# Identity built on chip, state rows first, two output blocks formed in place, sums respaced

## The chip, the cores and the metric

The kernel runs on one core of a Trainium2 chip. The metric is the device time of one execution in microseconds (us). Each core has five engines with queues of their own: TensorE (PE, with its weight loads PEld), VectorE (DVE), ScalarE (ACT), GpSimd (POOL) and SyncE (SP). They meet at semaphores. Transfers are issued from the queues of SP, ACT and POOL.

## The reference

Two operators follow each other. The first is a cross attention between 512 tokens and 32 state rows of each of 8 heads in each of 8 batches, in both directions; the second is a feed-forward layer over its 4352 output rows.

```python
B, H, S, Ns, D = (8, 8, 512, 32, 64)
a  = softmax(scale * x @ state.T);  xread = a  @ state
a2 = softmax(scale * state @ x.T);  sread = a2 @ x
rows = concatenate([xread, sread], axis=2)      # (B, H, 544, 64)
X = rows.transpose(0, 2, 1, 3).reshape(B * 544, 512)
h = X @ w_in                                    # d_ff = 2048
g = s * relu(h) ** 2 + b
out = g @ w_out                                 # float32
```

The scalar b only adds b times the column sums of w_out to every row. The kernel adds that as bias_bc.

## The kernel before

All work of a batch is done in tiles with 128 partitions, matmuls in fp16 with fp32 accumulation. Eight heads form two groups g of four (`head_of`).

*Attention.* The tokens of a batch (xn) are transposed to xT by TensorE for batches 0 and 1 (`att_xT_pe`, 16 transposes with the identity matrix ident16 as the moving operand, then copies to SBUF on VectorE, L197, and ScalarE) and by a DMA transpose for the others. The state rows are transposed in the same manner to stT (`att_stT`, copy at L157). `att_T` forms the scores T from stT and xT and their exponentials E. `att_D` multiplies E by the block matrix bones16, which gives the softmax denominators, and forms the shares a4. `att_M` folds the state rows into w_in: M = state times w_in, so that the layer's h comes straight from a4 and M (`mm1_x`, sixteen tiles f of 128 hidden units; two matmuls each). ScalarE applies the relu (L395). VectorE squares pairs of tiles into g (L405), but in batch 1 two pairs are squared by ScalarE (L403).

*Start.* For batch 0, x comes in two transfers xf (one per group) on SP's queue, the state rows of batch 0 and 1 in two transfers stf, one on ACT's queue and one on SP's. The matrix ident16 is an inline constant that ACT's queue loads first (L713). Each of these is cast to fp16: xf in four quarters (`cast_x0`, L742, on VectorE, ScalarE, VectorE and POOL), stf by POOL (`cast_st`, L734). POOL issues the transfers that cast while moving: four wi (w_in), four wo (w_out), xn of later batches, the remaining state rows. TensorE multiplies zeros (`warm_up`) until x is there, and between its first steps.

*Second matmul.* The first half of batch 0's tokens is multiplied by w_out directly (`mm2_part`). The other half of batch 0 ("0b") and every later batch use a 2 x 2 block scheme with seven products instead of eight (`fast_items`). Tokens are cut in two halves, hidden units in two, and output columns in two. `weight_sums` gives the differences t1 to t4 of w_out blocks (wd, eight VectorE subtractions, L490); `token_sum(b, i, j)` gives the sums s1 to s4 of g blocks, in two parts j each (L507 for i = 3, L512, L514, L516). The products p = 1 to 7 accumulate in three PSUM banks A, B and C. When a product is complete, `done` lets VectorE read the bank:

```python
p == 1: qa = A * s + bias          # L605
p == 6: u2 = B * s + qa            # L608
p == 7: u3 = B * s + qa            # L613;  qb = qa + bias_d   L616
p == 2: put("A", blk(0), 0, 0)     # osb = A * s + bias        L572
p == 5: put("C", u3, 1, NH)
p == 4: put("B", qb, 1, 0)
p == 3: put("C", u2, 0, NH)
```

Product 7 goes on adding into bank B after product 6, and product 4 after product 7. Each `put` writes an output block osb (a pool of three buffers), and POOL issues its transfer to out.

*Order.* TensorE, SP and POOL run in the order in which the program writes them down (`manual_schedule`); VectorE and ScalarE are placed by the scheduler, except where `issue_after` ties an instruction to another. The work is in stages: stage s runs `mm1_x(s, f)` for f = 0 to 15; beside them stand pieces of the attention of batch s + 1 (`pieces`) and the products of batch s - 1 (`items`). Stage 1 takes the rest of batch 0, at first direct units, then "0b" in f = 6 to 13. A dictionary in stage 1 says after which f the weight differences (`sums.pop(0)`) and the sums of "0b" are issued. G["last"] is the latest square or direct output on VectorE.

Of the kernel before, what the change touches and what calls it, by code (L numbers as in the profile page):

```python
# [14 lines left out]
def kernel(  # L15
# [72 lines left out]

    warm = konst.tile([P, 512], FP16, name="warm")
    ident16 = konst.tile([P, P], FP16, name="ident16")  # L90
    ident_dr = nc.inline_tensor(np.eye(P, dtype=np.float16), name="ident_const")
    bones16 = konst.tile([P, P], FP16, name="bones16")
    ones16 = konst.tile([P, Ns], FP16, name="ones16")
    mean16 = konst.tile([P, P], FP16, name="mean16")
# [77 lines left out]
    def new_xT(b):  # L172
        A[b]["xT"] = apool.tile([P, H, 2, P], FP16, name=f"xT_{b}", tag="xT")
        return A[b]["xT"]

    def att_xT_pe(b, g):
# [16 lines left out]
        xT = A[b]["xT"] if g else new_xT(b)  # L193
        dst = xT.rearrange("p (q g) k t -> p g q (k t)", g=NG)[:, g]
        for i in range(2):
            eng = nc.scalar.copy if i == 1 and (b, g) != (0, 1) else nc.vector.tensor_copy
            eng(  # L197
                dst[:, h2 * i : h2 * i + h2],
                two[i].rearrange("p (q t) -> p q t", q=h2),
            )  # L200

    def att_xT_dma(b):
        xT = new_xT(b)
# [184 lines left out]
    def mm1_close(key, hps, ntok, f):  # L388
        if f % 2 == 0:
            R2[key] = rpool.tile([P, 2, ntok], FP16, name=f"r_{key}_{f}", tag="r")  # L390
        r16 = R2[key]
        if key == 0 and f in (1, 5):
            nc.vector.tensor_scalar(r16[:, f % 2], hps, 0.0, None, ALU.max)
        else:
            nc.scalar.activation(r16[:, f % 2], hps, AF.Relu)  # L395
            G["relu"] = nc.cur_bb.bb.instructions[-1]
        if f % 4 == 0:
            G4[key, f // 4] = gpool.tile([P, 4, ntok], FP16, name=f"g_{key}_{f}", tag="g")
        gt = G4[key, f // 4]
        G[key, f] = gt[:, f % 4]  # L400
        if key == 1 and f in (5, 9):
            with tc.issue_after(nc.cur_bb.bb.instructions[-1]):
                nc.scalar.square(gt[:, f % 4 - 1 : f % 4 + 1], r16)  # L403
        elif f % 2 == 1:
            nc.vector.tensor_mul(gt[:, f % 4 - 1 : f % 4 + 1], r16, r16)  # L405
            G["last"] = nc.cur_bb.bb.instructions[-1]
# [111 lines left out]
    def fast_items(b):  # L518
# [41 lines left out]
        def put(bank, add, j, n0):  # L560
            if b == "sr":
                ends.append(own[1][:, len(ends) : len(ends) + 1])
                osb = ends[-1]
            else:
                osb = opool.tile([P, ni, NH], FP32, name=f"osb_{b}_{j}_{n0}", tag="osb")
            if bank == "C" and b == last_b:
# [35 lines left out]
        def done(p):  # L602
            if p == 1:
                q = keep("qa")
                nc.vector.scalar_tensor_tensor(q, acc["A"], s_bc, blk(NH), ALU.mult, ALU.add)  # L605
            elif p == 6:
                u = keep("u2")
                nc.vector.scalar_tensor_tensor(u, acc["B"], s_bc, kept["qa"], ALU.mult, ALU.add)  # L608
            elif p == 2:
                put("A", blk(0), 0, 0)  # L610
            elif p == 7:
                u = keep("u3")
                nc.vector.scalar_tensor_tensor(u, acc["B"], s_bc, kept["qa"], ALU.mult, ALU.add)  # L613
                d = bias_d.unsqueeze(1).broadcast_to([P, ni, NH])
# [43 lines left out]
    def bias_sum():  # L658
# [11 lines left out]
                )  # L670
        nc.vector.tensor_copy(wsum[:, 0], ps)
        nc.vector.tensor_sub(wsum[:, 1], ps, wsum[:, 0])
        A["wsum"] = wsum

    def bias_end():
# [34 lines left out]

    with tc.manual_schedule(engines={ET.PE, ET.SP, ET.Pool}):
        nc.vector.memset(warm, 0.0)
        nc.scalar.dma_start(ident16, ident_dr.ap())  # L713
        for g in range(NG):
            nc.sync.dma_start(
                xf[:, g],
                x[0, g :: NG].rearrange("h (q c) d -> q h (c d)", q=P),
            )
        nc.scalar.dma_start(stf[:, 0:2, :], st_v[:, 0:2, :])
        nc.scalar.preload_act_table_set("natural_log_exp_and_others")  # L720
        nc.sync.dma_start(stf[:, 2:4, :], st_v[:, 2:4, :])
        nc.sync.dma_start(sb_row[:, 0:1], moe_s.to_broadcast((1, 1)))
# [1 line left out]
        nc.gpsimd.memset(bones16, 0.0)  # L724
        for q in range(4):
            nc.gpsimd.memset(bones16[32 * q : 32 * q + 32, 32 * q : 32 * q + 32], 1.0)
        nc.gpsimd.memset(ones16, 1.0)
        nc.gpsimd.memset(mean16, 1.0 / Ns)
        nc.gpsimd.memset(one_row, 1.0)

        def cast_st(eng, b0, b1):
            n = 2 * (b1 - b0)
# [21 lines left out]
        nc.gpsimd.dma_start(out=st16[:, 4:, 0, :], in_=st_v[:, 4:, :])  # L754
        load_x(2)

        warm_up(11)
        cast_x0(0, 0, nc.vector.tensor_copy)
        cast_x0(0, 1, nc.scalar.copy)
        att_xT_pe(0, 0)  # L760
        att_stT(0)
        cast_x0(1, 0, nc.vector.tensor_copy)
        warm_up(2)
        att_T(0, [0])
        att_xT_pe(0, 1)
# [111 lines left out]
        for s in range(1, B):  # L877
# [16 lines left out]
            for f in range(NKF):  # L894
# [7 lines left out]
                if s > 1 and f in (4, 5):  # L902
                    with tc.issue_after(G["last"]):
                        token_sum(s - 1, 4, f - 4)
                if s in fast:
                    if f in ((10, 12) if s == 1 else (7, 11)):
                        with tc.issue_after(G["last"]):
                            token_sum(s, 3, int(f > 10))
                    if s == 1 and f in (13, 14):
                        with tc.issue_after(G["last"]):  # L910
                            token_sum(s, f - 12, 0)
                    if s > 1 and f in (11, 12):
                        token_sum(s, f - 10, 0)
                    if f == 15:
                        token_sum(s, 1, 1)
                        token_sum(s, 2, 1)
                for fn in todo_s.get(f, []):
                    fn()
                if s == 1:
                    with tc.issue_after(G["last"]):  # L920
                        for _ in range({0: 2, 1: 1, 2: 1, 6: 1, 7: 1, 8: 1, 9: 1}.get(f, 0)):
                            sums.pop(0)()
                        for i, j in {0: [(1, 0), (2, 0)], 1: [(1, 1), (2, 1)], 7: [(3, 0)], 8: [(3, 1)],
                                     10: [(4, 0), (4, 1)]}.get(f, []):
                            token_sum("0b", i, j)
                for fn in items[f]:
                    fn()
        rest = coming[last_b][16:]
        rows = fast_items("sr")

# [53 lines left out]
```

The softmax here doesn't subtract the row's maximum and nothing guards it: scores larger than these inputs give would overflow.

## Time and profile before

| What | Value |
|---|---|
| median of 4 executions | 209.08 us (208.62 to 209.66) |
| profiled execution | 209.45 us, of it 207.7 us from first to last instruction |
| TensorE busy | 197.9 us, 1971 matmuls |
| VectorE busy | 163.4 us, 286 instructions |
| ScalarE busy | 128.4 us |
| POOL busy | 38.7 us |
| granted TensorE clock | 0.998 |
| HBM | 17.33 MB read, 8.91 MB written |

Starts are counted in us from the first instruction. A timeline line gives start, duration, engine, line of the program, operation, the tiles written and read, shapes and count; in square brackets stands how long the engine had been idle, and what released it. A helper's line number (L70 for every matmul) says little, so matmuls are told by their tiles: h is `mm1_x`, T and D the attention, Mps `att_M`, oA, oB and oC the three banks of products, each with the batch's name behind it where it is 0b or sr (the state rows' output).

### The profile page before, as it was taken

The numbers are of one execution on the slowest core, as the hardware profiler recorded it, in microseconds if no ns is written. First come the engines' busy times: TensorE is split into PE (matmuls) and PEld (weight loads), VectorE is DVE, ScalarE is ACT, GpSimd is POOL, SyncE is SP. The second block draws the span as 40 slices with busy tenths as digits, with TensorE's granted clock in tenths as the row PEclk, the third lists the DMA queues.
The fourth block names the chain that finished last, engine by engine and source line by source line (L and its number), as shares of the span: only waits on it lengthen the run. The fifth ranks groups of instructions, "written<-read, shape, count | busy, mean of one in ns | idle before, by whom it ended". The sixth has DMA issues, their size and how long they took to land.

```text
span 207.7 us, 4853 instructions
## 1 busy us (share of the span) xinstructions
PE 197.9 (95%) x1971; PEld 132.5 (64%) x1971; DVE 163.4 (79%) x286; ACT 128.4 (62%) x254; POOL 38.7 (19%) x66
## 2 busy tenths in 40 slices
PE   7788899999999999999999999999999999999991
PEld 2334343556766676667676667676767777788881
DVE  0479779896959996799779966997699786796861
ACT  2478975699677666767676658675867555543100
POOL 5591001413210230023002101120112012100210
PEclk9999999999999999999999999999999999999999
DMA  5999997999999496929951934160416011200243
GB/s 177 226 201 206 206 191 104 181 189 176 158 157 191 101 179 92 200 73 208 139 103 54 151 109 104 51 158 3 101 47 157 11 51 51 103 2 0 79 139 92
DMA packets 46795, 25.55 MB, mean 123 GB/s; under 512 B 31732, under 2 KB 44788, under 8 KB 46772
## 3 DMA queue, kind: packets, MB, share of 16 engines
q0 software_dynamic: 15568, 16.19, 39.7%
q1 hardware_dynamic: 30180, 8.49, 23.9%
q10 hardware_dynamic: 1024, 0.56, 1.0%
q8 instruction: 15, 0.25, 0.5%
q14 instruction: 8, 0.07, 0.1%
HBM read 17.33 MB, written 8.91 MB: 126 GB/s over the span
## 4 chain that ended last, share of the span: by engine, by line
PE 84%; DMA 5%; DVE 3%; ACT 3%; issue 1%; POOL 1%; ACTq 0%
PE h L70 24%; PE oB L70 18%; PE oC L70 11%; PE oA L70 11%; PE Mps L70 4%; PE o L70 3%; PE h_sr L70 3%; DMA stf<-in_state_dram 3%; DMA a<-aT 2%; ACT r L395 2%; PE V L70 1%; PE oB_sr L70 1%; PE T L70 1%; PE oB_0b L70 1%; DVE M L320 1%
## 5 line engine op out<-in xcount | busy, mean ns | idle before, releaser
L395 ACT ACTIVATE r<-h 128x512 f16<-128x512 f32 x126 | 74.2, 602 | 44.2 <-PE h L70 44.2
L70 PE MATMUL h<-a,M 128*128 128x512 f16 x256 | 74.2, 379 | 1.2 <-DVE M L320 0.6
L70 PEld LDWEIGHTS <-s 128*128 128x128 f16 x448 | 43.7, 98 | 15.8
L405 DVE TENSOR_TENSOR g<-r 128x1024 f16<-128x1024 f16 x62 | 42.3, 683 | 12.3 <-ACT r L395 11.6
L70 PEld LDWEIGHTS <-g 128*128 128x128 f16 x392 | 37.3, 98 | 18.5 <-issue 4.4
L583 POOL DMA_DIRECT2D out_dram<-osb x27 | 18.2, 674 | 123.6 <-DVE osb L572 51.6
L70 PE MATMUL oB<-wd,s 128*128 128x256 f16 x224 | 32.8, 273 | 0.0
L70 PE MATMUL oA<-wo,g 128*128 128x256 f16 x224 | 32.5, 273 | 0.0
L70 PEld LDWEIGHTS <-M 128*128 128x128 f16 x256 | 24.3, 98 | 11.4 <-DVE M L320 1.6
L297 ACT CAST M<-Mps 128x1024 f16<-128x1024 f32 x20 | 20.1, 1006 | 0.0
L70 PE MATMUL oC<-wd,s 128*128 128x256 f16 x112 | 16.5, 273 | 0.0
L70 PE MATMUL oB<-wd,g 128*128 128x256 f16 x112 | 15.7, 273 | 0.0
L70 PE MATMUL oC<-wo,s 128*128 128x256 f16 x112 | 15.3, 273 | 0.0
L608 DVE SCALAR_TENSOR_TENSOR u<-oB,s_bc,qa 128x512 f32<-128x512 f32 x7 | 5.2, 750 | 7.5 <-PE oB L70 7.5
L395 ACT ACTIVATE r_sr<-h_sr 128x256 f16<-128x256 f32 x16 | 6.1, 382 | 7.9 <-PE h_sr L70 7.3
L234 ACT ACTIVATE E<-T 128x256 f16<-128x256 f32 x20 | 7.4, 384 | 4.0 <-PE T L70 4.0
L514 DVE TENSOR_TENSOR s<-s,g 128x1024 f16<-128x1024 f16 x14 | 9.6, 687 | 0.2
L70 PE MATMUL h_sr<-srdT,wi 128*128 128x256 f16 x64 | 9.6, 273 | 0.0
L507 DVE TENSOR_TENSOR s<-g 128x1024 f16<-128x1024 f16 x14 | 9.6, 686 | 0.0
L516 DVE TENSOR_TENSOR s<-g,s 128x1024 f16<-128x1024 f16 x14 | 9.6, 685 | 0.0
L512 DVE TENSOR_TENSOR s<-g,g 128x1024 f16<-128x1024 f16 x14 | 9.6, 684 | 0.0
L572 DVE SCALAR_TENSOR_TENSOR osb<-oC,s_bc,u 128x512 f32<-128x512 f32 x12 | 8.9, 745 | 0.4 <-PE oC L70 0.4
(126 smaller groups left out, 224.8 us busy)
## 6 DMA issues: line engine op xcount, KB each, us to landing
out_dram<-osb POOLq DMA_DIRECT2D x29, 256.0 KB, 2.8
xn<-in_x_dram POOLq DMA_DIRECT2D x7, 512.0 KB, 7.8
wi<-in_moe_w_in_dram POOLq DMA_DIRECT2D x4, 512.0 KB, 8.9
wo<-in_moe_w_out_dram POOLq DMA_DIRECT2D x4, 512.0 KB, 14.5
xf<-in_x_dram SPq DMA_DIRECT2D x2, 512.0 KB, 5.5
out_dram<-osb_0b POOLq DMA_DIRECT2D x4, 128.0 KB, 5.3
out_dram<-osb_sr SPq DMA_DIRECT2D x8, 32.0 KB, 1.6
out_dram<-osb_sr ACTq DMA_DIRECT2D x8, 32.0 KB, 1.7
```

What stands on the lines that cost most here:

```text
L70: return nc.tensor.matmul(out, lhsT, rhs, start=start, stop=stop, tile_position=tp, is_transpose=is_transpose, skip_group_check=True,)
L234: nc.scalar.activation(a["E"][:, g, 256 * m : 256 * m + 256], Ts[m][:, g, :], AF.Exp, scale=scale, accum_out=a["rs"][:, NG * m + g : NG * ...
L297: nc.scalar.copy(dst, ps)
L395: nc.scalar.activation(r16[:, f % 2], hps, AF.Relu)
L405: nc.vector.tensor_mul(gt[:, f % 4 - 1 : f % 4 + 1], r16, r16)
L507: nc.vector.tensor_sub(o, a11, a21)
L512: nc.vector.tensor_add(o, a21, a22)
L514: nc.vector.tensor_sub(o, SQ[b, 1, j], a11)
L516: nc.vector.tensor_sub(o, a12, SQ[b, 2, j])
L572: nc.vector.scalar_tensor_tensor(osb, acc[bank], s_bc, add, ALU.mult, ALU.add)
L583: nc.gpsimd.dma_start(dst[j][:, :, n0 : n0 + NH], osb)
L608: nc.vector.scalar_tensor_tensor(u, acc["B"], s_bc, kept["qa"], ALU.mult, ALU.add)
```

## The change

It has three parts. The identity is no longer loaded: VectorE writes 0 to 31 along the free axis by doubling, transposes it in 32 x 32 blocks, and compares the two in the four diagonal blocks of a zeroed tile. ACT's queue issues stf's first transfer before anything else. TensorE transposes the state rows of batch 0 after nine warm-up matmuls, ahead of two more and of xT; VectorE's cast of the second half of xf is tied behind its first xT copy. Three POOL memsets change places. Second, `put` for output rows j = 1 writes its result over the operand added (u3 or qb), and the transfer to out reads that tile. Third, ScalarE's two squares of batch 1 are those of f = 3 and 5 instead of 5 and 9; the weight differences, third and fourth sums of "0b" are issued at other f, two of them tied behind u2 and u3; the third sums of batch 1 move from stage 1 (f = 10, 12) to stage 2 (f = 1, 2).

```diff
-    ident_dr = nc.inline_tensor(np.eye(P, dtype=np.float16), name="ident_const")
+    lane_c = konst.tile([P, 32], FP16, name="lane_c")
+    lane_r = konst.tile([P, 32], FP16, name="lane_r")
...
+            xT_done[b, g, i] = nc.cur_bb.bb.instructions[-1]
...
-        if key == 1 and f in (5, 9):
+        if key == 1 and f in (3, 5):
...
+            elif j == 1:
+                osb = add
...
         nc.vector.memset(warm, 0.0)
-        nc.scalar.dma_start(ident16, ident_dr.ap())
+        nc.vector.memset(lane_c[:, 0:1], 0.0)
+        for w in (1, 2, 4, 8, 16):
+            nc.vector.tensor_scalar_add(lane_c[:, w : 2 * w], lane_c[:, 0:w], float(w))
+        nc.vector.transpose(lane_r, lane_c)
+        nc.vector.memset(ident16, 0.0)
+        for q in range(4):
+            blk32 = slice(32 * q, 32 * q + 32)
+            nc.vector.tensor_tensor(
+                ident16[blk32, blk32], lane_c[blk32], lane_r[blk32], ALU.is_equal
+            )
+        nc.scalar.dma_start(stf[:, 0:2, :], st_v[:, 0:2, :])
         for g in range(NG):
             nc.sync.dma_start(
...
-        nc.scalar.dma_start(stf[:, 0:2, :], st_v[:, 0:2, :])
...
+        nc.gpsimd.memset(one_row, 1.0)
+        nc.gpsimd.memset(mean16, 1.0 / Ns)
         nc.gpsimd.memset(ones16, 1.0)
-        nc.gpsimd.memset(mean16, 1.0 / Ns)
-        nc.gpsimd.memset(one_row, 1.0)
...
-        warm_up(11)
+        warm_up(9)
+        att_stT(0)
+        warm_up(2)
         cast_x0(0, 0, nc.vector.tensor_copy)
         cast_x0(0, 1, nc.scalar.copy)
         att_xT_pe(0, 0)
-        att_stT(0)
-        cast_x0(1, 0, nc.vector.tensor_copy)
+        with tc.issue_after(xT_done[0, 0, 0]):
+            cast_x0(1, 0, nc.vector.tensor_copy)
         warm_up(2)
         att_T(0, [0])
...
+                if s == 2 and f in (1, 2):
+                    with tc.issue_after(G["last"]):
+                        token_sum(1, 3, f - 1)
                 if s in fast:
-                    if f in ((10, 12) if s == 1 else (7, 11)):
+                    if s > 1 and f in (7, 11):
                         with tc.issue_after(G["last"]):
-                            token_sum(s, 3, int(f > 10))
+                            token_sum(s, 3, f // 8)
...
-                        for _ in range({0: 2, 1: 1, 2: 1, 6: 1, 7: 1, 8: 1, 9: 1}.get(f, 0)):
+                        for _ in range({0: 2, 1: 1, 2: 1, 3: 1, 6: 1, 9: 1}.get(f, 0)):
                             sums.pop(0)()
-                        for i, j in {0: [(1, 0), (2, 0)], 1: [(1, 1), (2, 1)], 7: [(3, 0)], 8: [(3, 1)],
-                                     10: [(4, 0), (4, 1)]}.get(f, []):
+                        for i, j in {0: [(1, 0), (2, 0)], 1: [(1, 1), (2, 1)], 3: [(3, 0)], 7: [(3, 1)]}.get(f, []):
                             token_sum("0b", i, j)
+                if s == 1 and f == 8:
+                    late_sum = sums.pop()
                 for fn in items[f]:
                     fn()
+                if s == 1 and f == 8:
+                    with tc.issue_after(G["u2", "0b"]):
+                        sums.pop(0)()
+                    sums.append(late_sum)
+                if s == 1 and f == 10:
+                    with tc.issue_after(G["u3", "0b"]):
+                        token_sum("0b", 4, 0)
+                        token_sum("0b", 4, 1)
```

G["last"] is now also set by the last step of `bias_sum`, and G["u2", b] and G["u3", b] name the instructions at L608 and L613.

More of the change, by code (lines that the diff above doesn't have):

```diff
@@ L174, in new_xT @@
         return A[b]["xT"]
+    xT_done = {}
     def att_xT_pe(b, g):
@@ L608, in done @@
                 nc.vector.scalar_tensor_tensor(u, acc["B"], s_bc, kept["qa"], ALU.mult, ALU.add)
+                G["u2", b] = nc.cur_bb.bb.instructions[-1]
             elif p == 2:
@@ L613, in done @@
                 nc.vector.scalar_tensor_tensor(u, acc["B"], s_bc, kept["qa"], ALU.mult, ALU.add)
+                G["u3", b] = nc.cur_bb.bb.instructions[-1]
                 d = bias_d.unsqueeze(1).broadcast_to([P, ni, NH])
@@ L672, in bias_sum @@
         nc.vector.tensor_sub(wsum[:, 1], ps, wsum[:, 0])
+        G["last"] = nc.cur_bb.bb.instructions[-1]
         A["wsum"] = wsum
```

## The prediction

> **What bounds the kernel now.** I read the page's busy shares first, then the chain of waits from its start, then the timelines of the two places where TensorE stands still.
>
> ```profile
> PE 197.9 (95%) x1971; PEld 132.5 (64%) x1971; DVE 163.4 (79%) x286; ACT 128.4 (62%) x254; POOL 38.7 (19%) x66
> ```
>
> TensorE sets the time, so an edit is worth what TensorE stops waiting for. It does not run packed in the first 27 us, and it has single gaps later. The first long piece of the chain (start, us, what) is a transfer:
>
> ```profile
> 1.17 6.08 DMA stf<-in_state_dram
> 7.25 0.05 issue
> 7.30 0.40 POOL st L734
> 7.70 0.70 POOL wi L126
> 8.40 0.78 POOL xn L742
> ```
>
> The state rows of batches 0 and 1 land at 7.25; everything before is waiting. The timeline (start, us, engine, line, what, idle before and its releaser) shows the same on the engines:
>
> ```profile
> 6.13 0.62 PE L70 MATMUL xTps<-ident,xn 128*128 128x128 f16 x8 [0.25 <-DVE xn L742]
> ...
> 6.79 0.59 ACT L197 COPY xT<-xTps 128x512 f16<-128x512 f16 x1 [0.52 <-PE xTps L70]
> ...
> 7.76 0.28 PE L70 MATMUL stTps<-ident,st 128*128 128x128 f16 x2 [1.00 <-POOL st L734]
> ...
> 8.43 0.30 PE L70 MATMUL T<-xT,stT 64*32 64x256 f16 x8
> ...
> 10.93 0.86 PE L70 MATMUL Mps<-wi,stT 64*32 64x512 f16 x8
> ```
>
> xT is complete at 7.38, yet the scores T start only at 8.43, because stT comes from the late state rows. The other place is batch 0's Strassen half:
>
> ```profile
> 42.74 0.49 PE L70 MATMUL oA_0b<-wo,g 128*128 128x256 f16 x3
> 43.72 0.60 PE L70 MATMUL oB_0b<-wd,s_0b 128*128 128x256 f16 x4 [0.48 <-DVE u_0b L608]
> ```
> ```profile
> 41.91 0.42 DVE L507 TENSOR_TENSOR s_0b<-g 128x512 f16<-128x512 f16 x1
> 42.25 0.69 DVE L490 TENSOR_TENSOR wd<-wo,wd 128x1024 f16<-128x1024 f16 x1
> 42.85 0.42 DVE L507 TENSOR_TENSOR s_0b<-g 128x512 f16<-128x512 f16 x1
> 43.18 0.48 DVE L608 SCALAR_TENSOR_TENSOR u_0b<-oB_0b,s_bc,qa_0b 128x256 f32<-128x256 f32 x1
> ```
>
> Product 7 keeps adding into bank B, so its first matmul waits until VectorE has read product 6 (u2, L608). Product 6 ended near 41.97, but VectorE was working off four subtractions. At the 0.108 us step of the neighbouring matmuls, TensorE would have gone on at 42.74 + 3 x 0.108 = 43.07; it went on at 43.72, so 0.65 us is lost.
>
> **The change part by part: the start.** ScalarE's queue no longer loads ident16 at 0.74; the state rows take its slot instead of 1.17. When they land decides the result, and this trace bounds it. Below, ident's 32 KB in that very slot took 3.4 us, to 4.14. The rows are 64 KB in 256-byte pieces, so they cannot be sooner. Above stands the present landing, 7.25.
>
> ```profile
> xf<-in_x_dram SPq DMA_DIRECT2D x1, 512.0 KB, 4.9
> ident<-ident_const ACTq DMA_DIRECT2D x1, 32.0 KB, 3.4
> ```
>
> Here a rule has to be weighed. The Trainium skill (DMA: Bandwidth & Descriptors, "Issuing engines are not separate DMA queues") says that transfers of all issuers interleave on the same 16 engines, so an issuer or a slot buys only sequencer time. By it the rows gain 1.17 - 0.74 = 0.43 us and land at 6.82. The DMA view of 2.7 to 4.5 us speaks otherwise:
>
> ```profile
> q1 hardware_dynamic: 600, 0.60, 95.3%
> q10 hardware_dynamic: 34, 0.01, 1.9%
> ```
>
> q10 is ScalarE's queue, q1 SyncE's. The rows had been issued by 1.76, and still only 34 of q10's packets moved, ident's stragglers among them, while xf's first half ran; from 4.5 to 6.0 q10 moved 255. They did not interleave with what had been issued before them: issue order decided. I therefore start from ident's landing: 8 more packets on the slowest DMA engine, each beside one of xf's (q10's and q1's packets take about 0.02 and 0.05 us there, 0.06 together, my estimate from those shares), so 4.14 + 8 x 0.06 = 4.65.
>
> TensorE's order also changes: warm-up 9, stT, warm-up 2, then xT of group 0. So xT now stands behind stT. From the landing: 0.05, cast 0.40, 0.05, stT 0.28, two warm-ups of 0.43, together 1.64 us until xT may start, and from xT to T 1.29 (6.13 to 7.42). T = landing + 2.93. At 4.65: stT at 5.15, xT at 6.29 rather than 6.13, T at 7.58, **0.85 us sooner**. VectorE takes the stT copy before the xT copy; it is ready at 5.5, so it holds nothing.
>
> Behind it: VectorE's cast of xf's second half was held by the stT copy until 8.29, and POOL's by the state cast and wi 2 until 8.39. Both now wait for xf itself (1.27 + 6.2 = 7.44), so xT of group 1 comes 0.9 sooner and D follows T. xf's first half has 32 KB more ahead of it; 0.15 us later still ends its cast at 6.23, under the 6.29. Next is wi 0: issued 1.98, landing after 8.0, at 9.98. M's first matmul moves from 10.93 to 10.08, just behind it: gain is capped at 0.95. The other weights have 0.5 us or more (wi 2 lands at 15.15 for a use at 15.7, xn of batch 1 at 17.8 for 18.3), so 0.85 goes through.
>
> The identity is 12 small VectorE instructions from 1.13. By the 128x1 copies (0.15) and the 128x256 copies (0.29) they cost 1.8 to 3.5 us, ending at 2.9 to 4.6; I take 0.2 each, 3.5. First use is 5.15, so nothing; past that, each us costs one. The skill speaks against this one too (SBUF — State Buffer, "Who interferes with whom"): a VectorE instruction in a two-port mode locks GpSimd out of writing descriptors. The five adds run while POOL issues wi 0 and 1 (1.98 to 3.65). By the rule that is at most 5 x 0.2 = 1.0, an issue end at 4.65; by the trace the software queue moves no packet between 2.7 and 4.5, and 9 until 6.0, so either way the sum is the same. POOL's three memsets merely swap places, off any path.
>
> **The differences.** In stage 1 VectorE has, between qa and u2, now only g of 7 and one subtraction: two of L490 (0.6 apart) and one of L507 (0.34) are moved. u2 can start when product 6 ends: **0.65 us**, all of it. What is moved ahead of the bias (one wd, one third sum, 0.94) takes the place of the square of tiles 2, 3 (0.6), which goes to ScalarE; bias_bc had 0.55 idle before it, so cover remains 0.2. ScalarE squares f = 3 instead of 9 (1.06): the relu of f = 4 moves from 36.42 to 37.1, ends 37.7, and the matmul that reuses its bank comes at 37.95: 0.25 left. At 44.03 ScalarE is freed of the same 1.06, in its packed stretch 41.6 to 53; E of batch 2, which releases D at 47.64, needs that to keep up. Late next are product 7's and 4's inputs: t4's second half now follows g of f = 9, ending near 45.2, with product 4 at 46.3; fourth sums near 46.7 for product 3 at 48.1. Batch 1's third sums go into stage 2 behind g of f = 1, at 56.7 to 57.9, where VectorE idled 1.28; u2 of batch 1 came at 58.09: nothing.
>
> **In place.** u3 and qb take their results; SCALAR_TENSOR_TENSOR stays 0.745. Bounds: 0 to 0.1 each, 16 instructions, under VectorE's 1.3 to 1.6 us of idle per stage. New waits: the next batch's u3 and qb wait for the output transfer. It lands in 2.8 us, the next writing comes some 13 us later; behind it on VectorE stand g and the sums, so it would show. I take 0.
>
> Sum: 0.85 + 0.65 = 1.50. The profiled execution is 207.7 of span and 1.75 around it, 209.45, hence 207.95; it stands 0.37 above the median of 209.08, which gives **207.6**. About that much is a single wait of this execution (a<-aT took 4.8 us at 112.9 where its others take 3.1), which I leave alone.
>
> **The rivals.** *State rows late (slower).* If the rows land at 6.82 by the rule, T is at 9.75 (+1.32), net +0.67; at 7.25, net +1.11. Time about 210.0. It decides from a landing of 5.50 (the start gains nothing) and 6.15 (the whole change gains nothing). For it: the rows' present landing. Against: ident in this slot. *The start is swallowed.* Rows at about 5.5, or wi 0 later: only 0.65 remains, 208.4. wi 0's 0.1 us of margin speaks for it. *The gap moves on.* E, t4 or a bank takes the place of u2: only 0.85, 208.2; for it ScalarE's packed stretch. *It does not do what it says*: neither comes, 209.1.
>
> **How the numbers follow.** Both parts 0.62 (207.6); swallowed 0.14; moved on 0.10; neither 0.05; rows late 0.09. About 0.5% is what measurement can tell, 1.05 us: faster is under 208.03. Main case mostly there (0.54 of 0.62), some of the next two (0.06): 0.60. Same: 0.30; slower: late rows beyond 210.1 and the unforeseen, 0.10. Low end: 0.95 + 0.65 and the a<-aT wait gone (0.5), 207.0, rounded to 206.9; high end takes in swallowed, moved on and neither, 209.2.
>
> **What would show it.** Right: the cast of st near 4.7, stT before 5.5, xT near 6.3, T near 7.6, M near 10.1 released by itself or wi; no idle before oB_0b product 7. Wrong: TensorE idle before stTps with POOL or stf as releaser, M waiting for wi past 10.3, or a wait at D or oB_0b in 42 to 50.

## The result and the profile after

The kernel after takes 209.19 us (median of 35 executions, 208.06 to 212.94) against 209.65 (56 executions, 208.62 to 213.76) for the kernel before on the same chips. The ratio is 0.9981 (0.9965 to 0.9997), a gain of about 0.4 us. A second series gave 209.39 against 210.01, ratio 0.9971 (0.9941 to 1.0001), about 0.6 us. The prediction said 1.50. The median time lies just inside the predicted range (206.9 to 209.2), in the part of it that had been kept for the rivals; the gain is a third of what was forecast. Of the executions, 8 of 35 after and 19 of 56 before took over 210 us: long executions are not something that the change brought. Medians and ranges here are of all executions; a ratio leaves out executions that stand far above the others of their kernel, so for kernels with a long tail the two differ.

The profiled execution of after lasted 212.94 us, of it 211.2 of span, the longest of its 35. It is read for its parts; its late waits need not stand in a usual execution. From the page, TensorE's row, the rows of busy tenths and granted clock:

```profile
PE 199.1 (94%) x1971; PEld 133.0 (63%) x1971; DVE 165.3 (78%) x298; ACT 128.4 (61%) x254; POOL 38.9 (18%) x66
...
PE   7888999999959999999999899999999999999991
...
PEclk9999999999969999999999999999999999999998
```

VectorE has the 12 instructions of the identity more. In slice 12 (58.1 to 63.4 us) TensorE is busy for half of the time, and its granted clock is down. Neither is in the page of before.

The start in the timeline of after (start, us, engine, line, what, idle before and its releaser):

```profile
5.24 0.40 POOL L752 CAST st<-stf 128x256 f16<-128x256 f32 x1 [1.52 <-DMA stf<-in_state_dram]
...
5.69 0.29 PE L70 MATMUL stTps<-ident,st 128*128 128x128 f16 x2 [0.48 <-POOL st L752]
...
6.24 0.61 PE L70 MATMUL xTps<-ident,xn 128*128 128x128 f16 x8
...
7.22 0.60 PE L70 MATMUL T<-xT,stT 64*32 64x256 f16 x8
...
9.99 0.86 PE L70 MATMUL Mps<-wi,stT 64*32 64x512 f16 x8
```

The state rows land 4.44 us after their issue, at 5.18 instead of 7.25. T stands at 7.22 (before 8.43) and M at 9.99 (before 10.93): 0.94 us sooner. At batch 0's half, TensorE and VectorE of after:

```profile
43.66 0.61 PE L70 MATMUL oB_0b<-wd,s_0b 128*128 128x256 f16 x4
...
46.49 0.82 PE L70 MATMUL oB_0b<-wd,g 128*128 128x256 f16 x6
47.65 0.27 PE L70 MATMUL oC_0b<-wo,s_0b 128*128 128x256 f16 x1 [0.35 <-DVE u_0b L578]
```
```profile
46.45 0.69 DVE L409 TENSOR_TENSOR g<-r 128x1024 f16<-128x1024 f16 x1 [0.66 <-ACT r L399]
47.06 0.16 DVE L340 RECIPROCAL rq<-rs 128x2 f32<-128x2 f32 x1
47.14 0.46 DVE L578 SCALAR_TENSOR_TENSOR u_0b<-oC_0b,s_bc,u_0b 128x256 f32<-128x256 f32 x1
```

The wait of 0.65 before product 7 is gone: oB_0b at 43.66 follows with no bracket. A new one stands before product 3, which writes bank C and must wait until VectorE has read product 5 out of it (L578). The last matmul of product 4 started at 46.49 + 5 x 0.108 = 47.03, so TensorE would have gone on at 47.14; it went on at 47.65, 0.51 later. VectorE was waiting 0.66 for a relu, for its square g, which stood in the queue ahead of that read. Before, the order was the other way (VectorE of before):

```profile
47.68 0.17 DVE L336 RECIPROCAL rq<-rs 128x2 f32<-128x2 f32 x1 [0.98 <-ACT E L243]
47.79 0.48 DVE L572 SCALAR_TENSOR_TENSOR osb_0b<-oC_0b,s_bc,u_0b 128x256 f32<-128x256 f32 x1
48.19 0.68 DVE L405 TENSOR_TENSOR g<-r 128x1024 f16<-128x1024 f16 x1
```

Product 3 starts at 48.72 before and 47.65 after: a lead of 1.07 us, which is 0.94 + 0.65 - 0.51 to 0.01. So 1.07 of the 1.50 arrives at 48 us, and the medians show 0.4 to 0.6 of it.

Two transposes by DMA matter from here on, both on SyncE's queue. xT<-xn turns the tokens of a batch for its scores T. In the later batches VectorE forms the shares on the transposed exponentials (ET<-E, another such transpose; den are their sums) and a<-aT turns the shares back for h. In this execution TensorE waits for the transposed x of batch 3 and for a<-aT of batch 5, and that takes back more than its whole lead:

```profile
60.22 0.65 PE L70 MATMUL T<-xT,stT 64*32 64x256 f16 x16 [2.46 <-DMA xT<-xn]
```
```profile
121.04 0.60 PE L70 MATMUL h<-a,M 128*128 128x512 f16 x2 [0.70 <-DMA a<-aT]
```

The same two of before:

```profile
58.65 0.40 PE L70 MATMUL T<-xT,stT 64*32 64x256 f16 x16
```
```profile
117.78 0.60 PE L70 MATMUL h<-a,M 128*128 128x512 f16 x2 [0.32 <-DMA a<-aT]
```

In before, T of batch 3 did not wait, and the second wait's bracket was 0.32. Measured between TensorE's matmuls with the step of 0.108 or 0.216, as above, the second is 0.49 before and 0.87 after; below, all such waits are measured so. The first cost more than its bracket, since TensorE's granted clock was down behind it (after, by stages: the columns are the stretch, its us, busy us of PE, PEld, DVE, ACT, POOL with counts, the granted clock, the DMA share and GB/s):

```profile
58.00:60.00 2.00, 0.00 (x0) 0.00 (x0) 0.97 (x2) 0.00 (x0) 0.00 (x0) 0.93 1.11 129
60.00:62.00 2.00, 1.78 (x28) 0.95 (x29) 0.00 (x0) 1.04 (x6) 0.00 (x0) 0.50 1.36 182
62.00:64.00 2.00, 2.00 (x13) 1.30 (x11) 0.98 (x3) 0.98 (x5) 0.65 (x1) 0.72 0.82 115
```

A small loss stands at the very end. The last transfer to out, before and after:

```profile
203.93 0.58 ACTq L597 DMA_DIRECT2D out_dram<-osb_last  x1
```
```profile
207.19 0.58 ACTq L603 DMA_DIRECT2D out_dram<-osb_last  x1
```

From its issue to the end of the span it is 3.74 us before and 3.97 after. In the seven traces of kernels with the old start (the identity loaded) it is 3.71 to 3.85, in the thirteen with the new one (the identity built, the state rows first) 3.85 to 4.23, on average 0.2 longer. What makes it longer is open.

### The profile page after: what moved, and what is told of

Its sections match the earlier page's. It is cut to its first block, busy times and chain, and to the rows that moved or that the text cites. A ratio compares the mean times of both kernels' runs of the same rounds, so it can differ in the third digit from the quotient of the medians.

```text
span 211.2 us, 4865 instructions
## 1 busy us (share of the span) xinstructions
PE 199.1 (94%) x1971; PEld 133.0 (63%) x1971; DVE 165.3 (78%) x298; ACT 128.4 (61%) x254; POOL 38.9 (18%) x66
## 4 chain that ended last, share of the span: by engine, by line
PE 79%; DMA 10%; ACT 4%; DVE 3%; issue 1%; POOL 0%; DVEq 0%
PE h L70 22%; PE oB L70 17%; PE oC L70 11%; PE oA L70 10%; DMA xT<-xn 6%; PE Mps L70 4%; PE o L70 3%; PE h_sr L70 3%; DMA a<-aT 2%; DMA stf<-in_state_dram 2%; ACT r L399 2%; PE T L70 1%; PE oB_sr L70 1%; PE V L70 1%; DVE M L324 1%; ACT M L327 1%
## 5 line engine op out<-in xcount | busy, mean ns | idle before, releaser
L589 POOL DMA_DIRECT2D out_dram<-osb x13 | 8.8, 673 | 73.9 <-DVE osb L578 34.2
L589 POOL DMA_DIRECT2D out_dram<-u x7 | 4.7, 677 | 42.3 <-DVE inv L284 28.1
```

The source lines that it names most:

```text
L589: nc.gpsimd.dma_start(dst[j][:, :, n0 : n0 + NH], osb)
```

## The experiments

### The parts, one at a time

Four kernels ran together: after again, before with the start alone (identity, order of transfers, warm_up and casts), before with the respacing alone, and before with the in-place blocks alone. The diff of the last:

```diff
+            elif j == 1:
+                osb = add
```

> The changed kernel once more, for a second trace. Theory A (the waits at the start and before product 7 are gone, 1.6 us in all, and later DMA waits give most of it back): TensorE's lead over the kernel before is about 1.1 us at 48 us (M of batch 0 near 10.0 instead of 10.9, a new wait of about 0.5 before product 3 of 0b), and the lead shrinks at T of batch 3 (xT by DMA) or at a later a<-aT; time 0.2 to 0.6 us under the kernel before. Theory C (nothing is lost later, the first trace was one bad execution): lead 1.1 us to the end, time 1.1 us under.

> Only the start: identity built by VectorE, state rows first, stT ahead of xT. M of batch 0 near 10.0. Theory A: 0.9 us won at 11 us, part of it lost after 45 us, time 0.2 to 0.6 under the kernel before. Theory C: the whole 0.9. Theory B (the output blocks formed in place cost what is missing): the whole 0.9 too, since nothing is formed in place here.

> Only the differences and sums respaced, with the square of f = 3 in place of f = 9 on ScalarE. The 0.65 us wait before product 7 of 0b goes; a wait of about 0.5 us before product 3 comes, because VectorE reads bank C late. Theories A, B and C: 0.1 to 0.2 us under the kernel before, nothing measurable. If it is over 0.4 slower, the respacing itself is what costs.

> Only the output blocks of j = 1 formed in place. Theory B: 0.4 to 0.8 us slower than the kernel before. Theories A and C: no difference (within 0.2 us).

Before, in this series, was 210.01. What the traces show is in the table (M: first M of batch 0; p3: product 3 of batch 0's half; waits in us):

| Kernel | Median | Ratio (interval) | M | p3 | wait at product 7 | at product 3 | at a<-aT of batch 5 |
|---|---|---|---|---|---|---|---|
| before | | | 10.93 | 48.72 | 0.65 | none | 0.49 |
| before, profiled again | 209.61 (one run) | | 10.73 | 48.52 | 0.64 | none | 0.45 |
| after again | 209.39 | 0.9971 (0.9941 to 1.0001) | 9.82 | 48.97 | none | 0.51 | 0.89 |
| start alone | 209.39 | 0.9963 (0.9933 to 0.9992) | 10.02 | 48.19 | 0.65 | 0.38 | 0.50 |
| respacing alone | 209.51 | 0.9979 (0.9944 to 1.0014) | 10.84 | 48.66 | none | 0.66 | 0.98 |
| in place alone | 209.46 | 0.9957 (0.9927 to 0.9988) | 10.70 | 48.49 | 0.65 | none | 0.85 |

After again had its granted clock at 0.5 for 3.4 us from 11.5, which is why its p3 is late. The medians cannot rank these parts: all four ratios lie within 0.0022 of each other. The traces can, up to 48 us. The respacing alone takes 0.65 away at product 7 and puts 0.66 at product 3: its worth is nothing. The start alone gives 0.91 at M against before, and 0.53 at product 3, where VectorE's read of bank C waited 0.71 for its output buffer (the profile names the transfer of osb as what released it). In the whole change that block is written in place, needs no buffer, and the wait is not there; so the in-place part, worth nothing by itself in its trace, seems to take away one thing that the earlier start would have met (start and respacing without it were not run together). The last column does not follow the change: two parts that leave the start as it was wait 0.85 and 0.98.

> The kernel before once more, for a second trace: how much of its picture (0.65 before product 7, no wait before product 3, 0.49 at h of batch 5 behind a<-aT) is the same in another execution. Theory A: 0.65 again; the wait at a<-aT between 0.3 and 1.0, depending on how long the instruction transfer beside it takes.

The second profile of before agrees with the first in every mark of the table to 0.2 us. Up to 48 us the marks are those of the kernel and not of one execution; the waits behind it vary more, as the parts show.

### The order at bank C

The read of bank C is tied ahead of the square of f = 11 and of batch 2's reciprocal:

```diff
+        elif key == 1 and f == 11:
+            def square_late():
+                with tc.issue_after(G["put5"]):
+                    nc.vector.tensor_mul(gt[:, f % 4 - 1 : f % 4 + 1], r16, r16)
...
-                at(11, lambda: att_ET(2))
+                if s == 1 and f == 11:
+                    with tc.issue_after(G["put5"]):
+                        att_ET(2)
+                    G["square_late"]()
```

> The changed kernel, with VectorE's read of bank C after product 5 (the put of j = 1, in place into u3) ahead of the square of f = 11 and of batch 2's reciprocal, and not behind them. If the wait of 0.51 before product 3 of 0b is that queue order: no wait there, product 3 about 0.5 us sooner relative to M of batch 0, TensorE 1.55 us ahead of the kernel before at 48 us, time 0.5 under the changed kernel. If ScalarE's packed stretch is the bound: the wait only moves to D, to h or to a later bank, time the same.

VectorE and TensorE of this kernel:

```profile
46.02 0.48 DVE L586 SCALAR_TENSOR_TENSOR u_0b<-oC_0b,s_bc,u_0b 128x256 f32<-128x256 f32 x1
46.42 0.15 DVE L340 RECIPROCAL rq<-rs 128x2 f32<-128x2 f32 x1
46.76 0.69 DVE L412 TENSOR_TENSOR g<-r 128x1024 f16<-128x1024 f16 x1 [0.19 <-ACT r L399]
```
```profile
47.46 0.27 PE L70 MATMUL oC_0b<-wo,s_0b 128*128 128x256 f16 x1
```

Product 3 no longer waits: it comes 37.16 us behind M instead of 37.66. Neither late instruction makes a new wait. So the 0.51 is settled as an order in VectorE's queue. But the median was 210.08 against 209.36 (ratio 1.0004, 0.9970 to 1.0037), with executions up to 215.21, although this trace had a span of 206.9, below those of before (207.7 and 207.8). Run again later:

> After with the order at bank C, again, as the reference of the two with a longer stream. Its first median (210.08) stood above before although its trace was the shortest. If that was chance, 208.8 to 209.2; if this order makes a loss that one trace does not show, 209.6 or more again.

It gave 208.79 against 209.65 (12 executions, 207.45 to 217.75; ratio 0.9929, 0.9890 to 0.9968). Half of the executions are below 208.7, and five are above 210. A lead that is there in one execution and gone in the next needs a cause of its own.

### TensorE's instruction stream and a<-aT

In the DMA view there are 15 transfers of 16 KB of kind "instruction" on q8. In every trace of a kernel with the stream unchanged, one of them ran beside a<-aT of batch 5. To move them against the rest, 27 small matmuls took the place of one warm-up, first in after, later in before:

```diff
-        warm_up(9)
+        for _ in range(27):
+            mm(tiny[0:32, 0:16], warm[0:64, 0:32], warm[0:64, 0:16], tp=(0, 0))
+        warm_up(8)
```

> The changed kernel with 27 tiny matmuls (32 x 16) in place of one warm-up: 52 more instructions in TensorE's stream, so that each 16 KB instruction transfer comes about 2.6 us earlier in the work. If the wait for a<-aT of batch 5 (0.5 to 0.9 us) is one DMA engine busy with such a transfer: no wait there, time 0.5 to 0.9 under the changed kernel, unless another a<-aT meets one (batch 7's window is the nearest). If it is the order of POOL's output transfer and a<-aT: the wait stays.

> The kernel before with 27 small matmuls in place of one warm-up, which shifts TensorE's instruction stream against the transfers. Theory F (the place of the stream decides the wait at a<-aT of batch 5, and what the shift does to batch 3's ET<-E): no wait at a<-aT of batch 5 (0.49 gone), a wait of 0.5 to 0.9 at oC of batch 2's stage near 70 us behind VectorE's denominator, as in after with the same stream; by the median within 0.3 us of before, and after with this stream is then 0.7 to 1.1 below it in the traces at 117 us. Theory G (the start's lead itself makes those transfers late): the a<-aT wait stays at 0.45 to 0.50 here and no wait comes near 70 us.

DMA views of the stretch 112 to 117.5 us; first before, then after again, then before with the longer stream (which has no q8 line there; the last column of an issue is us from issue to landing):

```profile
q8 instruction: 1, 0.02, 1.0%
...
a<-aT SPq DMA_TRANSPOSE x1, 4.8
```
```profile
q8 instruction: 1, 0.02, 1.8%
...
a<-aT SPq DMA_TRANSPOSE x1, 4.6
```
```profile
a<-aT SPq DMA_TRANSPOSE x1, 3.2
```

With the longer stream the first such transfer came at 14.9 instead of 19.2 us in before, so they do carry TensorE's instructions; a<-aT took 3.2 us, and the wait of h at 117 us was gone in both kernels. In before the median fell to 208.97 against 209.65 (ratio 0.9970, 0.9948 to 0.9992): some 0.6 us for an edit that computes nothing. In after it was 209.02 against 209.36 (0.9989, 0.9957 to 1.0020), because a new wait of 0.82 came at 69.28 behind VectorE's denominator of batch 3. VectorE and TensorE of after with the longer stream:

```profile
67.35 1.22 DVE L282 TENSOR_REDUCE den<-ET 128x32 f32<-128x1024 f16 x1 [1.86 <-DMA ET<-E]
68.48 0.74 DVE L578 SCALAR_TENSOR_TENSOR u<-oC,s_bc,u 128x512 f32<-128x512 f32 x1
```
```profile
69.28 0.60 PE L70 MATMUL oC<-wo,s 128*128 128x256 f16 x4 [0.65 <-DVE u L578]
```

It is the pattern of product 3 again: a read of bank C stands in VectorE's queue behind an instruction that waits for something else. Before with the same stream did not have that wait, against the expectation of Theory F, so the stream alone does not make it. That a<-aT meets an instruction transfer is shown as the cause of its wait; why the wait is 0.87 and 0.89 in the two traces of after and 0.45 to 0.50 in those of before is only partly seen. In after the denominator of batch 5 waits for its ET<-E, which took 6.2 us against 4.6 (VectorE of before and of after again):

```profile
109.04 1.21 DVE L278 TENSOR_REDUCE den<-ET 128x32 f32<-128x1024 f16 x1
```
```profile
109.86 1.22 DVE L282 TENSOR_REDUCE den<-ET 128x32 f32<-128x1024 f16 x1 [0.49 <-DMA ET<-E]
```

so aT is ready later and a<-aT is issued 3.8 instead of 4.4 us ahead of TensorE's need. But it varies by execution at least as much: with the stream unchanged, six traces with the old start had 0.25 to 0.98 (mean 0.58) and nine with the new start none to 1.58 (mean 0.64). That the change makes this wait longer is therefore not shown.

Both edits together, and the order with a stream longer by 9 and by 52 matmuls:

> The kernel after with both single gaps of its trace taken away: the order at bank C, and TensorE's stream lengthened by 51 small matmul instructions in place of one warm-up, so that its instruction transfer does not fall on a<-aT of batch 5. If single gaps in one trace add up to the time: 209.2 - 0.5 - 0.9 = about 207.9. If what one gap gives is taken back by the next late transfer (Theory A): 208.5 to 209.2, with a wait for a transposing transfer or an x load somewhere behind 55 us.

> After with the order at bank C and with 10 small matmuls in place of one warm-up: the stream is longer by 9 matmuls, the instruction transfers some 0.8 us earlier. Theory F: the transfer near 103 us falls ahead of ET<-E of batch 5, which lands in under 5 us (no wait at the denominator), and a<-aT still meets the next one: a wait of 0.3 to 0.6; time 208.6 to 209.1. Theory G: as with the order alone.

> After with the order at bank C and with 54 small matmuls in place of two warm-ups: the stream is longer by 52 matmuls, the instruction transfers some 8 us earlier in the middle stages. Theory F: the wait at a<-aT of batch 5 is gone, and so is that of batch 3's ET<-E near 69 us, whose transfer then comes near 52; a new one where another transpose now meets a transfer; 208.1 to 208.8. Theory G: a wait of 0.8 at a<-aT of batch 5 whatever the stream, 209.0 to 209.5.

They gave 208.88 against 209.78 (ratio 0.9953, 0.9895 to 1.0012), 208.58 against 209.65 (0.9949, 0.9914 to 0.9985) and 211.33 against 209.65 (0.9983, 0.9955 to 1.0011; six of its twelve executions above 212), where 208.1 to 208.8 had been expected. The wait at a<-aT was gone in all three traces, also with only 9 matmuls more, where a wait of 0.3 to 0.6 had been expected. The first had the wait near 69 us again (0.96). The other two had a wait at T of batch 3: 2.09 and 4.21 us. So a tail remains when the wait at a<-aT is gone, and this wait, seen in after too, is what could make it.

### The loads of x

The transpose xT<-xn of batch 3 runs beside POOL's loads of x for batches 4 and 5. First, the load of batch 4 was moved from f = 12 to f = 15 of stage 1, and that of batch 5 from f = 1 to f = 5 of stage 2; then the loads of batches 4 to 7 were left out, in three kernels:

```diff
-                at(12, lambda: load_x(4))
+                at(15, lambda: load_x(4))
-                at(1, lambda: load_x(5))
+                at(5, lambda: load_x(5))
```
```diff
     def load_x(b):
+        if b > 3:
+            xn[b] = xn[3]
+            return
         new_xn(b)
```

> The changed kernel with the loads of batch 4 and 5 issued later on POOL (after f = 15 of stage 1 and f = 5 of stage 2, instead of 12 and 1). If token loads that now run into the transposes of batch 3 cost time in most executions (theory A): xT of batch 3 lands 5 to 6 us after its issue, ET of batch 2 sooner, and the time is 0.3 to 0.6 under the changed kernel. If the 2.6 us wait was one bad execution: the same median.

> The kernel after with the x loads of batches 4 to 7 left out (those batches use batch 3's rows, so this part of the input is not read). Theory A (the 0.5 us that the traces of after gain by 48 us are eaten later by transfers that the x loads collide with: the transposes of x for batch 3, a<-aT): no wait at the scores T of batch 3 in 56 to 62 us, and against before without the same loads (its own run in this job) a gain of 0.8 to 1.1 us by the medians, with a narrower spread of times than with the loads. Theory B (the gain is eaten by VectorE's and ScalarE's order at product 3 and nothing else): the difference of the two stays at 0.3 to 0.5 us, whatever the loads. Both: the wait of 0.5 us at product 3 stays, since the loads have no part in it.

> The kernel before with the x loads of batches 4 to 7 left out in the same way. Theory A: the same as before to 0.5 us better (its transposes of x have slack, since TensorE comes later), 208.9 to 209.4. Theory B: the same as before. In both, the wait at product 7 of batch 0's half stays at 0.65, and that at a<-aT of batch 5 shows whether x loads take part in it: gone or under 0.2 if they do, 0.45 to 1.0 if TensorE's own instruction transfer causes it.

> The kernel after with VectorE's read of bank C tied ahead of the square of f = 11 and batch 2's reciprocal (as in the kernel with that order), and with the x loads of batches 4 to 7 left out. Theory A: 0.5 us under the kernel after without those loads, by the trace and by the median (with the loads, the trace showed that 0.5 and the median did not). Theory B: nothing against the kernel after without the loads, since the reciprocal taken later costs what the reading of bank C saves: a new wait at D or oA of batch 2's stage.

Moving both loads was worse: 210.58 against 209.36 (1.0028, 0.9998 to 1.0059). T of batch 3 did not wait, its transpose took 5.6 us, but the load of batch 5 now went out with xT<-xn of batch 4; SyncE's issue of that took 7.12 us, a<-aT of batch 3 behind it took 5.8 us instead of 3.1, and h waited 1.00 at 74.98. An instruction transfer of 1.40 us ran beside this a<-aT as well, so the share of the load in the wait is not separated; the load of batch 5 was left where it was from here on.

Without the loads, after was 209.11 (208.71 to 209.35, six executions), before 209.77 (209.38 to 211.82) and after with the order 208.89 (208.48 to 210.19); before with its loads 209.78 in that series. After is then 0.66 below before, and 0.88 with the order: between the two theories for the medians; the narrow range of after fits Theory A. T of batch 3 waited in none of the three. The wait at product 3 stayed (0.51) and so did that at a<-aT (0.57, 0.50 and 1.58): x loads have no part in them. Six executions each are few.

### The load and the transpose

All traces together show when the transpose is late. The columns are the issue of xT<-xn of batch 3 on SP, POOL's issue of the x load of batch 4 against it, and the transpose's time from issue to landing:

| Kernel | xT<-xn issued | load, against it | landing after |
|---|---|---|---|
| start alone | 46.44 | +2.52 | 6.7 |
| before; again; with the longer stream | 46.85; 46.98; 46.56 | +2.25; +2.18; +2.36 | 6.2; 8.5; 9.2 |
| in place; respacing alone | 46.95; 47.68 | +1.89; +1.75 | 6.6; 6.7 |
| after again; with the longer stream | 46.18; 46.75 | +3.56; +1.77 | 5.4; 6.5 |
| after | 47.33 | +1.09 | 12.8 |
| order and longer stream | 46.98 | +1.03 | 9.0 |
| order; again | 47.17; 46.65 | +0.15; +0.45 | 9.0; 8.4 |
| order, stream +9; +52 | 47.75; 48.72 | -0.43; -0.76 | 11.7; 13.5 |

A load 1.75 us or more behind the transpose goes with 5.4 to 9.2 us (5.6 where the load came 5.19 behind, 5.8 to 7.3 without the load), one within 1.1 us behind it with 8.4 to 12.8, one ahead of it with 11.7 and 13.5. The ranges overlap, so the distance is not all of it. An instruction transfer ran beside this transpose in every trace, late or not. The transpose's issue does not come earlier with TensorE's lead: it follows the load of batch 3, whose time TensorE does not set. The load of batch 4 stands on POOL's queue behind the transfer of batch 0's block from bank C, which VectorE now writes earlier. So the lead moves the load towards the transpose, and with the order at bank C past it in two traces. The last two experiments set that order by hand, in both directions:

```diff
-                at(12, lambda: load_x(4))
+                at(15, lambda: load_x(4))    # after with the order at bank C
...
-                at(12, lambda: load_x(4))
+                at(10, lambda: load_x(4))    # before
```

> After with the order at bank C, and the x load of batch 4 issued behind the last two output blocks of batch 0's half (near 52 us instead of 47). Theory L (load ahead of the transpose makes it late): xT<-xn of batch 3 lands within 7 us, no wait at T of batch 3, and the times lose their tail: 12 runs within 207.4 to 209.5, median 207.6 to 208.3. Theory R (the transpose is late by chance, whatever the load): the tail stays, about 4 of 12 runs above 210, median 208.8 as with the order alone. A third possibility: the load, now just ahead of batch 5's, lands too late for xT<-xn of batch 4 (issued near 61), and SyncE's queue holds a<-aT of batch 3: a wait of 0.5 to 1.0 near 75.

> The kernel before with the x load of batch 4 issued one output block earlier on POOL's queue (near 45.5 instead of 49.1), ahead of the transpose xT<-xn of batch 3 at 46.9. Theory L: that transpose takes 11 to 14 us, lands at 58 to 61 where TensorE wants it at 58.0, so T of batch 3 waits up to 3 us in many runs: median 210.0 to 211.5 and a tail above 212. Theory R: the same as before, 209.65 with its spread.

SP, POOL, the DMA view and TensorE, of before with the earlier load:

```profile
46.89 7.08 SPq L204 DMA_TRANSPOSE xT<-xn  x1
```
```profile
45.60 0.92 POOL L120 DMA_DIRECT2D xn<-in_x_dram  x1
```
```profile
xT<-xn SPq DMA_TRANSPOSE x1, 13.4
```
```profile
60.32 0.44 PE L70 MATMUL T<-xT,stT 64*32 64x256 f16 x16 [1.36 <-DMA xT<-xn]
```

and the same four of after with the order and the later load:

```profile
46.10 2.52 SPq L208 DMA_TRANSPOSE xT<-xn  x1
```
```profile
53.52 1.81 POOL L121 DMA_DIRECT2D xn<-in_x_dram  x2
```
```profile
xT<-xn SPq DMA_TRANSPOSE x1, 6.0
```
```profile
58.53 0.40 PE L70 MATMUL T<-xT,stT 64*32 64x256 f16 x16
```

With the load ahead of it, the kernel before, which has no lead, shows in its trace what after showed: 13.4 us, T waiting 1.54. It is the longest of its twelve executions. Its times do not show it: the median is 209.88 against 209.63 (1.0015, 0.9992 to 1.0037), below the 210.0 that had been the lower end of the expectation, no execution exceeded 212, and five of twelve exceeded 210, where before in that series had six of 23. With the load behind it, after with the order takes 6.0 us and no T waits. The tail is gone: twelve executions from 207.76 to 209.86, where the order alone had seven and five of twelve above 210. The median is 208.35 against 209.63, ratio 0.9951 (0.9926 to 0.9975), about 1.0 us by the ratio and 1.28 by the medians. This version is faster than before beyond its interval. Its ratio is also below that of after (0.9981, 0.9965 to 0.9997), but the intervals overlap and the two did not run together. No other with the change and all its loads stays as low in all of its executions.

Two things are shown, then: a load that goes out ahead of the transpose goes with 11.7 to 13.5 us in three of three traces, and with the order at bank C a load set behind it takes the tail away. That a late T takes part of the median of after is not shown: one of its two traces had it, in the longest of 35 executions, and its tail is no larger than that of before.

## Why the prediction was wrong, point by point

*The start: right in size, in part by luck.* Predicted 0.85 at M, measured 0.94 (9.99 against 10.93). The cap of 0.95 that wi 0 was to set did not hold: wi 0 came sooner too, at 9.62, and after again had M at 9.82, 1.11 sooner. The landing was mis-sized: 5.18, not 4.65. An opposite error made up for it, the path from there to T, 2.04 us instead of 2.93: from landing to xT 1.06 instead of 1.64 (the two warm-ups took 0.43 together, not each), so xT went at 6.24 (predicted 6.29), and from xT to T 0.98 instead of 1.29, so T went at 7.22, 0.36 ahead of the predicted 7.58. Of the 1.21 us that T came sooner, 0.27 was lost again before M. The rule of the Trainium skill (DMA: Bandwidth & Descriptors, "Issuing engines are not separate DMA queues") would have had the rows at 6.82; the earlier slot, with the identity's 32 KB gone from in front, was worth 2.07 us of landing, not 0.43. Slot and missing load were not tried apart. The gain is not there in every execution: three of the thirteen traces with the new start had M only at 10.94 to 11.46, as late as before or later (the last section).

*The identity: right.* The twelve instructions end at 3.25, in front of a first use at 5.69. POOL's issue of wi 0 and 1 ended at 3.72 against 3.65, so of the 1.0 us that was allowed for its being locked out at most 0.07 is seen.

*The differences: wrong. This is the step that the runs show to have failed.* "u2 can start when product 6 ends: 0.65 us, all of it" held only at product 7; at product 3 TensorE waited 0.51 that it had not waited before, so 0.14 was left. Tying the read of bank C ahead of the square took that wait away. The prediction had placed the fourth sums and product 3's input and named "a bank" as one of the ways the gap could move on, with 0.10 of chance; its sign of being wrong, a wait at D or oB_0b in 42 to 50 us, was set at other tiles than oC_0b, where the wait came. The prediction did not lay out VectorE's queue between u3 and the read of bank C, where the square of f = 11, waiting for its relu, had come ahead of that read. By itself, the respacing was worth 0.65 - 0.66, nothing.

*In place: right by itself, and not quite idle.* No cost was seen. In the whole change there is no sign of the wait for an output buffer that the start alone met at product 3 (0.71 on VectorE, 0.38 on TensorE).

*"A single wait of this execution (a<-aT ...), which I leave alone": wrong.* It is no single event: it is in all of the first ten traces but that with the longer stream, and TensorE's instruction transfers have a part in it. In both traces of after it took 0.4 more than in before, but over all traces with the stream unchanged it does not tell the new start from the old (means 0.64 and 0.58).

*What was not considered: the end of the kernel and POOL's queue.* Behind the last issue of a transfer to out, the new start costs 0.2 us in the traces, for a reason that stays open. As to POOL, the prediction followed the moved instructions on VectorE, ScalarE and TensorE, and asked of the lead only whether it would arrive. It did not ask what the lead itself moves. On POOL an x load follows the output block that now comes earlier; SyncE's transpose does not come earlier; and with the order at bank C the load gets there first in some executions. There it goes with a long tail; for after itself that is argued, not shown. The rival "the gap moves on" (208.2) was nearest in kind: the gap did move on to a bank, and took 0.51 of the 0.65.

The forecast sum, undone: 0.94 (start) + 0.65 - 0.51 (product 7, product 3) = 1.08 at 48 us; less 0.2 at the end leaves about 0.9; the medians show 0.4 and 0.6. Where the remaining 0.3 to 0.5 goes stays open. Three things that the traces show in single executions could take it: a late M, a longer wait at a<-aT, a late T. How often each came in the unprofiled executions is not seen.

## What to carry to other kernels

A gap that closes on one engine is worth its size only if the next read of every bank is followed through the reading engine's queue, instruction by instruction, with what each of those waits for. A lead moves only what hangs on the engine that has it: ask of every transfer behind it which others stand still, and tie the order of two that disturb each other instead of leaving it to chance. A median that does not show what the trace gains is a reason to look at the spread and at the trace of an execution from its upper end.

## What the runs showed of the hardware

TensorE's instructions come as 16 KB transfers, 15 in a run, each on one DMA engine for 0.9 to 2.7 us; beside one of them a<-aT of batch 5 took 4.3 to 5.9 us (15 traces), and 3.2 in the five with a longer stream, where none ran beside it or, in one, for its first 0.1 us alone. When TensorE had stood for 2.64 and for 4.21 us in front of T of batch 3, its granted clock was 0.5 for about the next 3.4 us; after 2.09 and 1.54 it was not. But after again had it at 0.5 for 3.4 us from 11.5 with no such wait in front. In three of the thirteen profiled executions with the new start, M came only at 10.94 to 11.46, about 1 us later than in the others: TensorE's warm-ups and the eight transposes of x still ran slowly at 6 to 7 us (0.94 to 1.06 us for the eight, 0.61 in the others). The page's clock row reads full there, but the trace's records of the granted clock begin only at 7.58, 7.66 and 9.66 us in these three, and at 4.1 to 6.4 in the other ten. In three of the seven traces with the old start the eight were as slow (0.94 to 1.06, first record at 6.64 to 7.48), and M still came at 10.70 to 10.76, since the scores there wait for the later state rows anyway. So the same slow start takes the gain away from the new kernel and nothing from the old one. M at 12.25, in before without the loads, is another case: its granted clock was recorded at 0.5 from 9.08 to 15.91. What decides when the full clock comes was not tried.
